# First expert's products in halves, a reordered tail and earlier records in a retention and mixture-of-experts kernel

## Chip, cores and metric

One core of a Trainium2 chip runs the whole program. The metric is the device time of one execution in microseconds; lower is better. Before the change it is 412.31 us (median of 3 runs, 411.94 to 412.67).

## What is computed

The reference first runs a retention (decayed linear attention) over 4 batches, 8 heads, 768 positions and 64 features, and then a mixture of experts in which each of the 3072 rows of 512 features goes to the one expert with the largest logit:

```python
intra = (qb @ kb^T * Dmask) @ vb ; inter = (qb * lam_pow) @ kv_state
kv_state = lam_block * kv_state + kb_dec^T @ vb
x = out.transpose(0, 2, 1, 3).reshape(3072, 512)
logits = x @ w_gate ; e_idx = argmax(logits)
for e in range(8):
    h = relu(x[e_idx == e] @ w1[e])          # 512 -> 1024
    out[e_idx == e] = gate_w * eom[:, e] * (h @ w2[e])   # 1024 -> 512
```

`gate_w` is the softmax weight of the chosen expert and `eom` a sigmoid of a second gate.

## The kernel before

The rows are cut into 24 tiles of 128 (six chunks of positions by four batches, `NTILE = 24`, `B = 4`, `RES = 16`, `LAST = 20`). A loop over steps `s` runs the retention of one tile a step, software-pipelined: `stage_a` turns keys and queries on TensorE, `stage_b` and `stage_b2` make the decayed scores, `stage_c1` and `stage_c` make the output x (`xT`, features on partitions) and the state, and `stage_d2` turns x back with VectorE and stores it to `x_d` in device memory. The order of instructions is the order of the Python calls (`tc.manual_schedule`), on each engine's queue.

Routing runs beside it by groups of tiles: `logits` (TensorE), `logit_rows` (a transpose and, for the last two groups, a sum `lg`), `route_choose` (VectorE: `mx`, `pl`, `cm`, `oh`; then two exponentials on ScalarE and the *record* of each row on GpSimd, an `IOTA` and a `TENSOR_SCALAR` that write the row's number and its place in `x_d` into `rec`), and `route_place` (rank products `pr` on TensorE, then about eleven small VectorE steps that end in the slot `sl`, the index `idx` and the weight in `rec`). `place_scatter` writes each tile's records to a table in device memory, `tab_d`, with one indirect DMA of GpSimd per tile. The groups are four tiles each up to tile 19, then tiles 20 and 21 (`LAST`), then 22 and 23 (`LAST + 2`).

The expert with the most rows so far is found before the last tiles are done (`pick_first`, from the counts of the first 16 tiles), so its weights load early: `load_piece(i)` loads the i-th piece of 1 MB, pieces 0 and 1 being the halves of its first matrix, 2 and 3 those of the second (`raw`). Rows of that expert come in two ways. Those of the first 16 tiles come from `tab_d` and a search (`mark`, `found`, `row_turn`, `row_index`, `row_join`) and are gathered in steps 18 to 21 by eight indirect DMAs of GpSimd, 32 rows each (`gather(0, ...)`, line 894; tiles `xg_0`, `xg_1`, four gathers each). Ahead of every second gather stands a hold, `pace`, a copy of one element of `xT` to `beat` on GpSimd (line 841). The remaining rows of the expert come in six gathers at the end (`xg_2`, `xg_3`), behind the late search `pfound_late`. `x_turn(0, i)` turns a tile `xg_i` on VectorE into `y` (line 911).

The first expert's products are a list of 48 `units`: 32 products of `up_mm` (8 column blocks `fc` by 4 feature blocks `kc`, line 945, 128x128 weights from `raw` against the 256 columns of `y_0`, in plain float32, two matmul records each) and 16 of the second matrix. `fill(n)` takes the next n units and `settle(n)` runs the relu steps (`up_act`) of completed blocks. The tail after the loop, from line 1302, interleaves both with the last routing by hand; its lines before the first expert's own loop are:

```python
x_turn(0, 0); logits(LAST + 2, 2); x_turn(0, 1); stage_d2(n - 3, 2)
load_piece(2); fill(3)
for f in place[1:]: f()
place_scatter(len(pending)); logit_rows(LAST + 2); fill(6)
```

Behind the six late gathers the second piece of the first expert's rows (`ys[(0, 1)]`, 192 columns) is multiplied, again at line 945, and from there on TensorE runs one expert after the other. PSUM has eight banks, taken in turn (`bank`).

Of the kernel before, what the change touches and what calls it, by code (L numbers as in the profile page):

```python
# [9 lines left out]
F32 = mybir.dt.float32  # L10
# [13 lines left out]
def kernel(  # L24
# [446 lines left out]
    def logits(n0, nb):  # L471
        parts = P // EG // nb
        pl = bank(f"pl_{n0}")
        for i in range(NPAIR // parts):
            for b in range(nb):
                xTv = xTs.pop((n0 + b)) if i == NPAIR // parts - 1 else xTs[n0 + b]
                xTv = xTv.rearrange("p (g t) -> p g t", g=NPAIR)
                for k in range(parts):
                    g = k * (NPAIR // parts) + i
                    r = (b * parts + k) * EG  # L480
                    nc.tensor.matmul(
                        pl[r : r + EG, 0:P], wgs[:, g, :], xTv[:, g], start=(i == 0), stop=(i == NPAIR // parts - 1)
                    )
        lT = small.tile([P, P], F32, tag="lT", name=f"lT_{n0}")
        nc.scalar.copy(out=lT, in_=pl[:, 0:P])
        lgs[n0] = (pl, lT, nb, parts)
# [41 lines left out]
    routed = {}  # L528

# [9 lines left out]
    def route_choose(n0, n1):  # L539
# [21 lines left out]
        rec = sm("rec", [P, nb, 3], I32)  # L561
# [6 lines left out]

        def record():
            nc.gpsimd.iota(rec[:, :, 0], pattern=[[S, nb]], base=b0 * S + c * P, channel_multiplier=1)  # L570
            nc.gpsimd.tensor_scalar(
                out=rec[:, :, 2], in0=row0[:, b0 : b0 + nb], scalar1=float(c * B * P * 4), scalar2=None,
                op0=ALU.add,
            )
# [9 lines left out]
            lambda: (exps(), record()),  # L584
# [353 lines left out]
    def up_mm(p, fc, h, kc):  # L938
        sl = slice((fc % 4) * P, (fc % 4 + 1) * P)
        r = cols(p, h)  # L940
        if kc == 0:
            phs[(p, fc)] = bank(f"ph_{p}_{fc}_{h}")
        if p == 0:
            nb = min(8, NB[p] - 8 * h)
            nc.tensor.matmul(  # L945
                phs[(p, fc)][:, r].rearrange("p (b r) -> p b r", b=nb),
                raws[fc // 4][:, kc, sl],
                ys[(p, h)][:, 0 : nb * P].rearrange("p (b g r) -> p g b r", b=nb, g=NPAIR)[:, kc],
                start=(kc == 0),
                stop=(kc == NKC - 1),  # L950
            )
            return
# [223 lines left out]
    for fc in range(NFC):  # L1176
        for kc in range(NKC):
            act = (lambda fc=fc: up_act(0, fc, 0)) if kc == NKC - 1 else None
            units.append((lambda fc=fc, kc=kc: up_mm(0, fc, 0, kc), act))
# [16 lines left out]
    with tc.manual_schedule():  # L1196
        ranking = []
        late = []
        STORES = {4: 0, 6: 2, 8: 4, 9: 6, 11: 8, 13: 10, 14: 12, 16: 14, 20: 16, 21: 18}
# [9 lines left out]
        for s in range(-2, NTILE - 2):  # L1209
# [64 lines left out]
            if s == 5:  # L1274
                number_tables()
            if s >= 0:
# [14 lines left out]
            if s >= RES + 2:  # L1291
                pace(xTs[s][0:1, 0:1])
# [3 lines left out]
                if s == RES + 5:  # L1296
                    load_rows(0, 2, None, nc.gpsimd)
                    load_piece(1, nc.gpsimd)
            if s < RES:
# [24 lines left out]
        x_turn(0, 1)  # L1324
        stage_d2(n - 3, 2)
        load_piece(2)
        fill(3)
        for f in place[1:]:
            f()
        place_scatter(len(pending))  # L1330
        logit_rows(LAST + 2)
        fill(6)
        at_once(route_choose(LAST + 2, NTILE))
        for b in range(2):
            mark(LAST, b, 1, late_width)
        last = route_place(LAST + 2, NTILE)
        counts = rank_counts("pcount")
        last[0]()
        fill(6)
# [4 lines left out]
        for b in range(2):  # L1344
            mark(LAST + 2, b, 1, late_width)
        pfound = bank("pfound_late")
        for n in range(RES, NTILE):
            found(pfound, n, (n - RES) // B + 1, late_width, n == RES, n == NTILE - 1)
        settle(2)
# [3 lines left out]
        fill(5)  # L1353
        row_turn(2, pfound, late_width)
        row_index(0, 2)
# [41 lines left out]
        for p in range(E):  # L1397
# [5 lines left out]
            for fc in range(NFC):  # L1403
# [21 lines left out]
                if p == 0 and fc < 2:  # L1425
                    next_rows(1, 10 + 2 * fc, 12 + 2 * fc, hts[(p, fc)][0][0:1, 256:257].bitcast(F32))
# [196 lines left out]
```

## Time and profile before

| | before |
|---|---|
| median of 3 runs | 412.31 us (411.94 to 412.67) |
| the profiled execution | 413.83 us |
| its span, first to last instruction | 412.2 us |
| TensorE (PE) busy | 397.1 us, 96% |
| VectorE (DVE) busy | 280.3 us, 68% |
| ScalarE (ACT) busy | 184.0 us, 45% |
| GpSimd (POOL) busy | 233.0 us, 57% |
| mean granted clock of TensorE | 0.993 |

The profile is of one execution. Times in its rows are microseconds from the start of the span unless marked ns; a row of the timeline has the start, the length, the engine, the line of the kernel, the operation, the output and inputs, how many instructions are merged (x), and in brackets the idle time before it and what ended that. A busy TensorE also counts time in which a product runs at a lower clock, so the clock is read apart, in the views by stretch.

### The profile page before, as it was taken

To read this page: it belongs to the slowest core of one execution; us is meant where nothing else is said; L and a number is where in the kernel's file an instruction comes from. 1 tells how busy PE (TensorE), PEld (TensorE's weight loads), DVE (VectorE), ACT (ScalarE), POOL (GpSimd) and SP (SyncE) were. 2 spreads that over 40 slices of the span, in tenths; PEclk is the share of its full clock that TensorE was granted. 3 is DMA by queue.
4 is the path that set the end of the run, shared out by engine and by line. 5 is a ranking of instruction groups with operands and counts; after the bars stand their busy time and mean duration, and the time that the engine had idled before them with its cause. 6 is when DMAs were issued, how large, how long until landed. Compare 5 with 4: busy or idle time off the path is not lost.

```text
span 412.2 us, 10314 instructions
## 1 busy us (share of the span) xinstructions
PE 397.1 (96%) x3767; PEld 364.2 (88%) x3767; DVE 280.3 (68%) x798; ACT 184.0 (45%) x450; POOL 233.0 (57%) x305
## 2 busy tenths in 40 slices
PE   8999989799969999999999999999999999999995
PEld 5879978688858898999999999999999989989985
DVE  3858786678867639778669757957965874863611
ACT  3757656578413325446045325604713542542500
POOL 2567877755876777874583666376386266211002
PEclk9999999999989999999999999999999999999998
DMA  9999999998968844744369648757946985461001
GB/s 179 225 206 254 230 220 233 254 224 198 286 196 249 242 164 105 241 147 139 127 185 308 220 130 237 242 183 188 320 151 172 300 258 167 129 214 64 0 26 48
DMA packets 102116, 78.96 MB, mean 192 GB/s; under 512 B 66348, under 2 KB 78128, under 8 KB 102064
## 3 DMA queue, kind: packets, MB, share of 16 engines
q1 hardware_dynamic: 93264, 63.85, 55.5%
q0 software_dynamic: 6544, 14.15, 11.1%
q10 hardware_dynamic: 2256, 0.30, 0.5%
q8 instruction: 30, 0.49, 0.5%
q14 instruction: 22, 0.18, 0.2%
HBM read 62.45 MB, written 16.21 MB: 191 GB/s over the span
## 4 chain that ended last, share of the span: by engine, by line
PE 75%; DMA 12%; SPq 6%; DVE 3%; issue 1%; POOL 1%; ACTq 0%; POOLq 0%; DVEq 0%
PE ph_None L83 10%; PE ph_None L82 10%; PE ph_None L81 10%; PE py L82 6%; PE py L83 6%; PE py L81 6%; PE pyr L82 4%; PE pyr L81 4%; PE pyr L83 4%; SPq L175 3%; PE ps L389 3%; PE ph L945 3%; SPq L168 3%; DMA tab_d<-rec,idx 3%; PE po L433 2%; DMA xg<-x_d,rows 2%
## 5 line engine op out<-in xcount | busy, mean ns | idle before, releaser
L894 POOL DMA_INDIRECT xg<-x_d,rows x103 | 114.5, 1112 | 63.7 <-issue 34.7
L971 ACT ACTIVATE hhi<-ph_None 128x400 fp32r<-128x400 f32 (+4 forms) x56 | 28.1, 501 | 120.5 <-PE ph_None L83 115.6
L136 DVE TENSOR_TENSOR wlo<-raw,whi 128x512 fp32r<-128x512 f32 x120 | 79.6, 684 | 0.7 <-ACT whi L127 0.5
L83 PE MATMUL ph_None<-xhi,wlo 128*128 128x400 f32 (+4 forms) x224 | 76.3, 341 | 0.0
L81 PE MATMUL ph_None<-xhi,whi 128*128 128x400 f32 (+4 forms) x224 | 76.3, 341 | 0.0
L82 PE MATMUL ph_None<-xlo,whi 128*128 128x400 f32 (+4 forms) x224 | 76.3, 341 | 0.0
L127 ACT CAST whi<-raw 128x512 fp32r<-128x512 f32 x120 | 70.0, 614 | 0.0
L977 DVE SCALAR_TENSOR_TENSOR hlo<-ph_None,hhi 128x400 fp32r<-128x400 f32 (+4 forms) x56 | 31.8, 568 | 37.2 <-ACT hhi L971 37.0
L398 DVE TENSOR_TENSOR at<-ps,decay 128x512 f32<-128x512 f32 x48 | 31.2, 683 | 22.5 <-PE ps L389 22.2
L83 PE MATMUL py<-hhi,wlo 128*128 128x400 f32 (+2 forms) x128 | 44.6, 348 | 0.0
L82 PE MATMUL py<-hlo,whi 128*128 128x400 f32 (+2 forms) x128 | 44.6, 348 | 0.0
L81 PE MATMUL py<-hhi,whi 128*128 128x400 f32 (+2 forms) x128 | 44.6, 348 | 0.0
L81 PEld LDWEIGHTS ph_None<-xhi,whi 128*128 128x128 f32 x224 | 42.1, 188 | 0.4
L82 PEld LDWEIGHTS ph_None<-xlo,whi 128*128 128x128 f32 x224 | 42.1, 188 | 0.4
L83 PEld LDWEIGHTS ph_None<-xhi,wlo 128*128 128x128 f32 x224 | 42.1, 188 | 0.3
L1092 POOL DMA_INDIRECT out_dram<-yn,table x12 | 13.3, 1112 | 49.5 <-DVE yn L1165 31.9
L349 ACT COPY qT<-pq 64x256 f32<-64x256 f32 x88 | 34.7, 394 | 2.5 <-PE pq L341 1.7
L81 PE MATMUL pyr<-whi,hhi 128*128 128x512 f32 (+1 forms) x88 | 34.6, 393 | 0.0
L82 PE MATMUL pyr<-wlo,hhi 128*128 128x512 f32 (+1 forms) x88 | 34.3, 390 | 0.0
L83 PE MATMUL pyr<-whi,hlo 128*128 128x512 f32 (+1 forms) x88 | 34.3, 390 | 0.0
L699 POOL DMA_INDIRECT tab_d<-rec,idx x24 | 24.6, 1024 | 14.9 <-DVE rows L853 4.5
L945 PE MATMUL ph<-y,raw 128*128 128x256 f32 (+1 forms) x128 | 26.9, 369 | 3.4 <-issue 3.2
(211 smaller groups left out, 717.2 us busy)
## 6 DMA issues: line engine op xcount, KB each, us to landing
raw<-in_moe_w_dram SPq DMA_DIRECT2D x31, 1024.0 KB
x_d<-xn SPq DMA_DIRECT2D x12, 512.0 KB
qkv<-in_k_dram SPq DMA_DIRECT2D x38, 128.0 KB
qkv<-in_v_dram SPq DMA_DIRECT2D x19, 256.0 KB
qkv<-in_q_dram SPq DMA_DIRECT2D x36, 128.0 KB
yd<-yo SPq DMA_DIRECT2D x12, 256.0 KB
yr<-yd SPq DMA_DIRECT2D x48, 64.0 KB
xg<-x_d,rows POOLq DMA_INDIRECT x103, 3.4
```

The costliest lines, as they stand in the source:

```text
L81: nc.tensor.matmul(ps, a[0], b[0], start=first, stop=False)
L82: nc.tensor.matmul(ps, a[0], b[1], start=False, stop=False)
L83: nc.tensor.matmul(ps, a[1], b[0], start=False, stop=last)
L127: nc.scalar.copy(out=hi, in_=src)
L136: eng.tensor_tensor(out=lo, in0=src, in1=hi.bitcast(F32), op=ALU.subtract)
L349: copies = [lambda r=r, view=view, src=src: nc.scalar.copy(out=view(qT[r]), in_=src) for r, view, src in query_parts(pq)]
L398: nc.vector.tensor_tensor(out=at, in0=ps.rearrange("p (g t) -> p g t", g=NPAIR), in1=dec[:, j], op=ALU.mult)
L699: nc.gpsimd.indirect_dma_start(out=tab_d, out_offset=bass.IndirectOffsetOnAxis(ap=idx, axis=0), in_=rec, in_offset=None, bounds_check=P * ...
L894: nc.gpsimd.indirect_dma_start(out=xg[(p, b // 4)][:, (b % 4) * P : (b % 4 + 1) * P], out_offset=None, in_=x_q[0 : 4 * rows], in_offset=ba ...
L945: nc.tensor.matmul(phs[(p, fc)][:, r].rearrange("p (b r) -> p b r", b=nb), raws[fc // 4][:, kc, sl], ys[(p, h)][:, 0 : nb * P].rearrange(" ...
L971: nc.scalar.activation(out=hi[:, r], in_=ph[:, r], func=AF.Relu)
L977: nc.vector.scalar_tensor_tensor(out=to, in0=ph[:, r], scalar=0.0, in1=hi[:, r].bitcast(F32), op0=ALU.max, op1=ALU.subtract,)
```

## The change

Five things are changed. The first 16 of the first expert's products are issued as 32 products of 128 columns: the halves that need `xg_0` alone first, then those of `xg_1`. The tail is put in another order. The records of the groups of tiles 12, 16, 20 and 22 are made in steps 6, 7, 9 and 10, in tiles of their own (`rec_...` in `const`). Piece 2 of the weights, which Sync loaded in the tail, is loaded by GpSimd directly behind piece 1. The holds at the early gathers and at the last four gathers of the second expert are removed. `lT` also gets one buffer in place of two.

```diff
-        lT = small.tile([P, P], F32, tag="lT", name=f"lT_{n0}")
+        lT = small.tile([P, P], F32, tag="lT", bufs=1, name=f"lT_{n0}")
...
+    recs = {}
+    def record(rec, n0, nb):
+        c, b0 = divmod(n0, B)
+        nc.gpsimd.iota(rec[:, :, 0], pattern=[[S, nb]], base=b0 * S + c * P, channel_multiplier=1)
+        nc.gpsimd.tensor_scalar(
+            out=rec[:, :, 2], in0=row0[:, b0 : b0 + nb], scalar1=float(c * B * P * 4), scalar2=None, op0=ALU.add
+        )
+    def early_record(n0, nb):
+        recs[n0] = const.tile([P, nb, 3], I32, name=f"rec_{n0}")
+        record(recs[n0], n0, nb)
...
-            lambda: (exps(), record()),
+            lambda: (exps(), None if known else record(rec, n0, nb)),
...
-    def up_mm(p, fc, h, kc):
+    def up_mm(p, fc, h, kc, part=None):
...
+            if part is not None:
+                nb, y0, r = 4, 4 * P * part, slice(P * part, P * part + P)
...
-    for fc in range(NFC):
-        for kc in range(NKC):
-            act = (lambda fc=fc: up_act(0, fc, 0)) if kc == NKC - 1 else None
+    for part, fcs in ((0, range(4)), (1, range(4)), (None, range(4, NFC))):
+        for fc in fcs:
+            for kc in range(NKC):
+                act = (lambda fc=fc: up_act(0, fc, 0)) if kc == NKC - 1 and part != 0 else None
...
+        EARLY_RECORDS = {6: (RES - B, B), 7: (RES, B), 9: (LAST, 2), 10: (LAST + 2, 2)}
...
+            if s in EARLY_RECORDS:
+                early_record(*EARLY_RECORDS[s])
...
             if s >= RES + 2:
-                pace(xTs[s][0:1, 0:1])
                 gather(0, 2 * (s - RES - 2) + 1, 2 * (s - RES - 2) + 2, RES * P)
...
                     load_piece(1, nc.gpsimd)
+                    load_piece(2, nc.gpsimd)
...
         logits(LAST + 2, 2)
-        x_turn(0, 1)
-        stage_d2(n - 3, 2)
-        load_piece(2)
-        fill(3)
+        fill(8)
         for f in place[1:]:
             f()
-        place_scatter(len(pending))
-        logit_rows(LAST + 2)
-        fill(6)
-        at_once(route_choose(LAST + 2, NTILE))
         for b in range(2):
             mark(LAST, b, 1, late_width)
+        place_scatter(len(pending))
+        x_turn(0, 1)
+        logit_rows(LAST + 2)
+        fill(8)
+        at_once(route_choose(LAST + 2, NTILE))
+        stage_d2(n - 3, 2)
         last = route_place(LAST + 2, NTILE)
+        fill(4)
         counts = rank_counts("pcount")
         last[0]()
-        fill(6)
+        fill(4)
         stage_d2(n - 1, 2)
         load_piece(3)
...
             mark(LAST + 2, b, 1, late_width)
+        fill(10)
         pfound = bank("pfound_late")
...
-        settle(2)
...
         place_scatter(len(pending))
-        fill(5)
+        settle(1)
+        row_index(0, 2)
+        fill(2)
         row_turn(2, pfound, late_width)
-        row_index(0, 2)
         row_join(2, late_width)
...
-                    next_rows(1, 10 + 2 * fc, 12 + 2 * fc, hts[(p, fc)][0][0:1, 256:257].bitcast(F32))
+                    next_rows(1, 10 + 2 * fc, 12 + 2 * fc)
```

On TensorE, at the end of the last logits (`pl`) and the start of the first expert's products (`ph_0` is block 0, `y_0` holds eight gathered pieces), before:

```order
L481 MATMUL pl_2607<-xT_2565,wgs 32x128 x2
L945 MATMUL ph_0_0_2625<-y_0_2605,raw_2390 128x256 x3
L492 MATMUL pl_2607<-ident,lT_2616 128x128
L945 MATMUL ph_0_0_2625<-y_0_2605,raw_2390 128x256
L945 MATMUL ph_1_0_2651<-y_0_2605,raw_2390 128x256 x4
L945 MATMUL ph_2_0_2656<-y_0_2605,raw_2390 128x256
```

and with the change:

```order
L481 MATMUL pl_2608<-xT_2569,wgs 32x128 x2
L953 MATMUL ph_0_0_2619<-y_0_2606,raw_2394 128x128 x4
L953 MATMUL ph_1_0_2624<-y_0_2606,raw_2394 128x128 x4
L492 MATMUL pl_2608<-ident,lT_2617 128x128
L953 MATMUL ph_2_0_2654<-y_0_2606,raw_2394 128x128 x4
L953 MATMUL ph_3_0_2659<-y_0_2606,raw_2394 128x128 x4
L953 MATMUL ph_0_0_2619<-y_0_2606,raw_2394 128x128 x4
```

Sixteen half products of blocks 0 to 3 now stand ahead of the first that needs the second four pieces, and eight instead of three products stand ahead of the transpose of the last logits.

On VectorE, at the turns of `xg_0` and `xg_1` into `y_0`, before:

```order
L583 TENSOR_TENSOR oh_2461<-pl_2530,cm_2584 128x16
L911 STREAM_TRANSPOSE y_0_2605<-xg_0_2153 128x512
L911 STREAM_TRANSPOSE y_0_2605<-xg_1_2373 128x512
L516 STREAM_TRANSPOSE xn_2619<-xT_2379 128x512
L516 STREAM_TRANSPOSE xn_2619<-xT_2468 128x512
L672 TENSOR_REDUCE pr_2601<-ex_2585 128x2
```

and with the change, from the end of the placing of tiles 20 and 21 (which now follows the turn of `xg_0` at once):

```order
L672 RECIPROCAL rec_1191<-den_2598 128x2
L651 TENSOR_REDUCE oh_2639<-oh_2464 128x8
L601 TENSOR_SCALAR marks_2641<-slot_no,lead_142,sl_2599 128x192 x2
L917 STREAM_TRANSPOSE y_0_2606<-xg_1_2377 128x512
L496 TENSOR_REDUCE lg_2652<-pl_2608 128x32
L583 TENSOR_REDUCE mx_2664<-lg_2652 128x2
L584 TENSOR_TENSOR pl_2608<-lg_2652,mx_2664 128x16
L585 SCALAR_TENSOR_TENSOR pl_2608<-pl_2608,erev 128x16
L588 TENSOR_REDUCE cm_2665<-pl_2608 128x2
L589 TENSOR_TENSOR oh_2639<-pl_2608,cm_2665 128x16
L516 STREAM_TRANSPOSE xn_2675<-xT_2383 128x512
```

The turn of `xg_1` moved behind the placing and the marks of tiles 20 and 21, and the x transposes moved behind the choosing for tiles 22 and 23.

On GpSimd, from the load of piece 1 on (`DMASW0` to `DMASW7` are the semaphores of its DMAs, each used by every eighth one in turn, so that a DMA waits for the landing of the one eight places ahead; `tab_d<-rec,idx` is a scatter), before:

```order
L114 DMA raw_2485<-in_moe_w_dram 128x4x512 [waits DMASW2_49]
L699 DMA tab_d<-rec_2358,idx_2372 24576x3 [waits DMASW3_49,DMASW1_49,DVE_49]
L699 DMA tab_d<-rec_2358,idx_2372 24576x3
L841 COPY beat<-xT_2565 1x1 [waits Activation_49,Pool_49]
L699 DMA tab_d<-rec_2358,idx_2372 24576x3 [waits DMASW5_49]
L699 DMA tab_d<-rec_2358,idx_2372 24576x3 [waits DMASW6_49]
L570 IOTA rec_2587 128x2
L571 TENSOR_SCALAR rec_2587<-row_136 128x2
L699 DMA tab_d<-rec_2587,idx_2600 24576x3 [waits DMASW7_49,DVE_49,Pool_49]
L699 DMA tab_d<-rec_2587,idx_2600 24576x3 [waits DMASW0_49]
L570 IOTA rec_2662 128x2
L571 TENSOR_SCALAR rec_2662<-row_136 128x2
```

and with the change, to the last scatter:

```order
L114 DMA raw_2487<-in_moe_w_dram 128x4x512 [waits DMASW2_49]
L114 ISA
L114 DMA raw_2489<-in_moe_w_dram 128x4x512 [waits DMASW3_49]
L705 DMA tab_d<-rec_955,idx_2376 24576x3 [waits DMASW1_49,DVE_49]
L705 DMA tab_d<-rec_955,idx_2376 24576x3 [waits DMASW5_49]
L847 COPY beat<-xT_2569 1x1 [waits Activation_49,Pool_49]
L705 DMA tab_d<-rec_955,idx_2376 24576x3 [waits DMASW6_49]
L705 DMA tab_d<-rec_955,idx_2376 24576x3 [waits DMASW7_49]
L705 DMA tab_d<-rec_1191,idx_2601 24576x3 [waits DMASW0_49,DVE_49]
L705 DMA tab_d<-rec_1191,idx_2601 24576x3
L705 DMA tab_d<-rec_1282,idx_2682 24576x3 [waits DMASW2_49,DVE_49]
L705 DMA tab_d<-rec_1282,idx_2682 24576x3 [waits DMASW3_49]
```

Both records left the row of scatters, a second weight piece stands ahead of it, and the first scatter waits in both for the semaphore DMASW1, that of the small read of `index_2` from `tab_d` just ahead of the weights; the last scatter now has the semaphore DMASW3, used last by piece 2.

## Rows read from the trace of the kernel before

**Rows 1.** The page: its first line.

```profile
span 412.2 us, 10314 instructions
```

**Rows 2.** The waits of TensorE from 100 us on: in total, times, longest.

```profile
PE ph L945 <- issue: 3.2, 1, 3.2
```

**Rows 3.** Timeline of TensorE, 100 to 160 us.

```profile
114.30 0.65 PE L481 MATMUL pl<-xT,wgs 128*32 128x128 f32 x16
118.17 1.57 PE L945 MATMUL ph<-y,raw 128*128 128x256 f32 x6 [3.23 <-issue]
...
126.76 0.25 PE L602 MATMUL pfound_late<-marks,row_lo 128*128 128x192 bf16 x1
...
128.08 7.53 PE L945 MATMUL ph<-y,raw 128*128 128x256 f32 x34
...
146.69 10.64 PE L945 MATMUL ph<-y,raw 128*128 128x192 f32 x64 [0.15 <-DVE y L911]
```

**Rows 4.** The chain that ended last, 100 to 160 us: start, length, what.

```profile
114.76 2.58 DMA xg<-x_d,rows
...
138.44 7.63 DMA xg<-x_d,rows
```

**Rows 5.** Timeline of VectorE, 100 to 160 us.

```profile
114.10 0.71 DVE L911 STREAM_TRANSPOSE y<-xg 128x512 f32<-128x512 f32 x1
...
118.00 1.26 DVE L516 STREAM_TRANSPOSE xn<-xT 128x512 f32<-128x512 f32 x2
...
120.47 0.21 DVE L496 TENSOR_REDUCE lg<-pl 128x32 f32<-128x64 f32 x1
...
121.56 0.17 DVE L583 TENSOR_TENSOR oh<-pl,cm 128x16 bf16<-128x16 f32 x1
...
124.27 0.18 DVE L663 TENSOR_TENSOR pr<-pr,ebase 128x16 f32<-128x16 f32 x1 [0.85 <-PE pr L633]
...
125.40 0.74 DVE L977 SCALAR_TENSOR_TENSOR hlo<-ph,hhi 128x256 fp32r<-128x256 f32 x2
...
129.50 0.23 DVE L876 TENSOR_TENSOR rows<-found,rows 128x4 int32<-128x4 f32 x2
...
146.10 0.45 DVE L911 STREAM_TRANSPOSE y<-xg 128x256 f32<-128x256 f32 x1 [3.60 <-DMA xg<-x_d,rows]
```

**Rows 6.** Busy time by stretch: length, PE, PEld, DVE, ACT, POOL, granted clock, DMA share, GB/s.

```profile
119.00:123.00 4.00, 4.00 (x13) 3.22 (x12) 3.76 (x22) 0.69 (x3) 3.23 (x5) 0.57 1.12 378
...
118.00:132.00 14.00, 13.83 (x72) 11.91 (x73) 10.79 (x54) 3.24 (x9) 9.60 (x14) 0.88 0.99 297
20.00:60.00 40.00, 38.60 (x854) 34.00 (x851) 28.34 (x90) 25.20 (x69) 30.45 (x48) 1.00 0.96 231
```

**Rows 7.** The same chain as rows 4, transposes of queries.

```profile
100.68 0.44 PE pq L341 x4
```

**Rows 8.** Timeline of GpSimd, 96 to 172 us.

```profile
109.64 0.74 POOL L571 TENSOR_SCALAR rec<-row 128x4 int32<-128x4 f32 x1
...
114.42 0.18 POOL L841 COPY beat<-xT 1x1 f32<-1x1 f32 x1
114.76 1.02 POOL L894 DMA_INDIRECT xg<-x_d,rows  x1 [0.16 <-DMA tab_d<-rec,idx]
...
116.44 0.84 POOL L114 DMA_DIRECT2D raw<-in_moe_w_dram  x1
118.65 1.07 POOL L699 DMA_INDIRECT tab_d<-rec,idx  x1 [1.37 <-DVE y L911]
...
129.09 0.99 POOL L699 DMA_INDIRECT tab_d<-rec,idx  x1 [0.30 <-issue]
131.37 1.07 POOL L894 DMA_INDIRECT xg<-x_d,rows  x1 [1.29 <-DVE keys L745]
```

**Rows 9.** Timeline of Sync's queue, 96 to 172 us.

```profile
134.54 4.22 SPq L114 DMA_DIRECT2D raw<-in_moe_w_dram  x2
```

**Rows 10.** DMA issues from 124 to 127 us: count, median us to landing.

```profile
tab_d<-rec,idx POOLq DMA_INDIRECT x2, 8.0
```

More of the change, by code (lines that the diff above doesn't have):

```diff
@@ L560, in route_choose @@
         ex, ez = sm("ex", [P, nb, E]), sm("ez", [P, nb, E])
-        rec = sm("rec", [P, nb, 3], I32)
+        rec = recs.pop(n0) if n0 in recs else sm("rec", [P, nb, 3], I32)
+        known = n0 >= RES - B
         routed[n0] = (oh, ex, ez, rec)
@@ L567, in exps @@
             nc.scalar.activation(out=ex, in_=d, func=AF.Exp)
[L569 to L574, printed above, removed]
         return [
@@ L936 @@
     hts = {}
-    def up_mm(p, fc, h, kc):
+    def up_mm(p, fc, h, kc, part=None):
         sl = slice((fc % 4) * P, (fc % 4 + 1) * P)
         r = cols(p, h)
-        if kc == 0:
+        if kc == 0 and not part:
             phs[(p, fc)] = bank(f"ph_{p}_{fc}_{h}")
         if p == 0:
-            nb = min(8, NB[p] - 8 * h)
+            nb, y0 = min(8, NB[p] - 8 * h), 0
+            if part is not None:
+                nb, y0, r = 4, 4 * P * part, slice(P * part, P * part + P)
             nc.tensor.matmul(
@@ L947, in up_mm @@
                 raws[fc // 4][:, kc, sl],
-                ys[(p, h)][:, 0 : nb * P].rearrange("p (b g r) -> p g b r", b=nb, g=NPAIR)[:, kc],
+                ys[(p, h)][:, y0 : y0 + nb * P].rearrange("p (b g r) -> p g b r", b=nb, g=NPAIR)[:, kc],
                 start=(kc == 0),
@@ L1175 @@
     acts = []
-    for fc in range(NFC):
-        for kc in range(NKC):
-            act = (lambda fc=fc: up_act(0, fc, 0)) if kc == NKC - 1 else None
-            units.append((lambda fc=fc, kc=kc: up_mm(0, fc, 0, kc), act))
+    for part, fcs in ((0, range(4)), (1, range(4)), (None, range(4, NFC))):
+        for fc in fcs:
+            for kc in range(NKC):
+                act = (lambda fc=fc: up_act(0, fc, 0)) if kc == NKC - 1 and part != 0 else None
+                units.append((lambda fc=fc, kc=kc, part=part: up_mm(0, fc, 0, kc, part), act))
     for j in range(2):
```

## The prediction

> **What bounds the kernel now.** I start with the page: the span is 412.2 us [rows 1]; the profiled execution took 413.83 us, so 1.6 us lie outside the span. The list of TensorE's waits comes next. From 100 us to the end it names one idle time worth a step, 3.2 us before the first expert's products (line 945) [rows 2]; the only other at that line is 0.15 us before their second piece, at 146.69 [rows 3]. Behind that the list has nothing: one unbroken stream of products, so whatever moves the start of the second piece moves the end by as much, as long as nothing later runs dry.
>
> The timeline of TensorE shows the hole: the last logits start at 114.30 us and end near 114.9, and the first product starts at 118.17 [rows 3]. It waited for the *second* half of its 256 rows: a product takes 8 gathered pieces at once, pieces 4 to 7 landed at 117.34 [rows 4], and VectorE turned them then, while the first four had been turned from 114.10 to 114.81 [rows 5]. Then the clock: from 119 to 123 us the granted clock is 0.57 on average, that is 1.2 of 2.4 GHz for most of it [rows 6]. Before it fell, the engine had stood idle for those 3.2 us and had been busy again for about one. So 4 x 0.43 = 1.7 us more are lost there.
>
> But TensorE is one of two chains that meet at 146.69. The other is the second piece of rows: its last gather is issued at 138.44 and lands 7.63 us later [rows 4], VectorE turns it at 146.10 [rows 5], and TensorE goes on 0.15 us after it had run out of other work. Both chains must become shorter, or the gain of the first is lost at the second.
>
> **The change part by part.** *Halves.* The first 16 products become 32 of 128 columns, and the first 16 of those need only the turn that ends at 114.81. TensorE starts at 114.9 instead of 118.17: **-3.3 us**. Without that idle time I expect the clock to stay up: **-1.7 us**. Each half loads its weights again. Rows on both sides: the four 128-column products of a transpose take 0.44 us, 0.11 each [rows 7], and the 34 records of 256 columns 7.53 us, 0.22 each [rows 3] (a product is two records). By these two halves cost what one whole does, and I take 0. The dear end is that a half record is no cheaper than one of 192 columns, 10.64 / 64 = 0.166 us [rows 3]: 64 x 0.166 - 32 x 0.22 = +3.6 us. I stay at the cheap end because the 0.11 is measured on the same 128 columns with a new 128x128 load for each. The Trainium skill (TensorE: Matmul & The Clock Gate, Back-to-back issue gap) speaks against the halves: in a stream of load and product it gives about 81 ns for 128 columns where the product alone would take 56. By that factor of 1.45 the halves would cost about 3 us more, an estimate from that page; rows 7 do not show it. TensorE would now run out of other work at 146.54 - 3.3 - 1.7 = **141.6 us**.
>
> *Reordered tail, VectorE.* The turn of pieces 4 to 7 goes behind the placing of the last-but-one pair of tiles and its marks. Laid out by durations: the placing takes 1.2 us (119.26 to 120.47 [rows 5]) and ends at 116.0, the marks at 116.6, the turn at 117.3, the choosing (120.47 to 121.73 [rows 5]) at 118.6, four x transposes at 0.63 each [rows 5] at 121.1, three placing steps and marks (124.27 to 125.40 [rows 5]) at 122.3. TensorE needs the turn at 114.9 + 16 x 0.22 = 118.4 and the marks at about 123.2: a margin near 1 us in both places. The 16 "found" products take 1.3 us (126.76 to 128.08 [rows 3]) and end at 124.5; the row numbers, ready at 129.73 before [rows 5], come at about 125.4, over 4 us earlier. The first x store moves 0.7 us back, to 120, the second 2.2 us forward, to 121.2; both are before the gathers by far more than they need.
>
> *Holds and records, GpSimd.* The removed one-element copies hold nothing back: the one at 114.42 starts as its gather ends and the next gather follows 0.34 us behind that, where two DMAs in a row stand 0.30 apart [rows 8]. I cost them at nothing. The record of tile group 16 took 0.74 us of arithmetic plus its index fill between two gathers [rows 8]; without it the last of the early gathers moves from 114.76 [rows 8] to about 113.7. The eight late scatters start from 118.65 to 129.09 [rows 8], 10.4 us for seven steps, where a scatter of 0.99 and a gap of 0.30 [rows 8] would make 9.1: the two records between them cost 1.3 us. Their new place is in steps 6 to 10, where GpSimd has 30.5 busy us in 40 and TensorE waits for others [rows 6]; I cost them at nothing, and at most 4 x 0.9 us if TensorE had to wait for each.
>
> *Weight piece 2 on GpSimd's queue.* It adds a 0.84 us issue there [rows 8]. In its favour, the next scatter waits anyway, as the order shows, for the small index read; the raw issue ended at 117.28 and the scatter started at 118.65 [rows 8]. The index read moves forward with the gathers, so the first scatter comes at about 117.5 and the last at 129.09 - 1.15 - 1.3 = 126.6. SP loses one issue and its next piece is no longer behind piece 2. That is later than the row numbers (125.4): GpSimd's queue is **late next**. From the last scatter to the first gather went 2.28 us, 129.09 to 131.37 [rows 8], of which 1.0 has no releaser that I can name. With it the gather chain moves by 2.45 us, without it by 3.4. Its landing is the unknown: 2.58 us when nothing else is in flight, 7.63 when a weight piece issued at 134.54 and the next one 4 us later run beside it [rows 4, 9]. SP's pieces move forward too, since they wait for the scatters and for buffers that TensorE's pace frees, so the race stays about as it was. At 7.63 the second piece starts at 143.3 to 144.2; at 2.58 it starts when TensorE is ready, at 141.6. I take 143.2, near the middle: 146.69 - 143.2 = **3.5 us gained**. The single buffer for lT costs nothing; its two uses are 3 us apart.
>
> The sum against the profiled execution: 413.83 - 3.5 = 410.3. The median of the runs is 412.31, 1.5 lower, so **408.8 us**.
>
> **The rivals.** (A) *The halves are dear.* At the 192-column price, +3.6 us, TensorE arrives at 145.2, behind the gathers: 412.3 - 1.5 = 410.8. For it: each half loads its weights anew; against it: the 0.11 us of rows 7. Chance 0.08.
> (B) *The clock falls all the same*, at the wait of up to 2 us that is left before the second piece, or in the tail: 1.7 us come back, 410.5. For it: it fell once after an idle time [rows 6]; against: that one was longer. Chance 0.10.
> (C) *The change does not do what it says*, because the weight piece is dear on GpSimd: from 116.44 to 118.65 went 2.21 us [rows 8], and if that was the issue itself and not the index read, piece 2 adds 2.2 us. Then the last scatter is at 128.8, close to before, the gathers hardly move, TensorE waits for them, and the time is about 412. Chance 0.12.
> (D) *Slower.* The scatters share a queue with 2 MB of weights, and the last one waits, as the order shows, for the landing of piece 2 (DMASW3). From 118 to 132 us 297 GB/s were moved [rows 6], 4.2 MB: about three weight pieces and two x stores. If piece 2 is served last, it lands at 117.3 + 14 = 131.3. Then the last scatter is at 131.6, the first gather 2.28 later, the last 7.07 behind that at 141.0, and it lands at 148.6: TensorE starts at 149.2, 2.5 us later than now, 414.8, and 1.7 more if the clock falls. It decides from the point at which the last gather lands behind 146.1 us. For it: scatters took 8.0 us to land beside such traffic [rows 10]. Against: pieces 1 and 2 are issued before the x stores and have a head start of 3 us. Chance 0.07. The Trainium skill (DMA: Bandwidth & Descriptors, Issuing engine by pattern and Arbitration) also speaks against this edit: plain loads belong on Sync, and an engine takes turns between queues but serves one queue in order. By that rule the scatters land behind both pieces; this trace, with only piece 1 on that queue, cannot show the second.
>
> **How the numbers follow.** My forecast has 0.63, with a range of its own from 407.3 (TensorE ready at 141.6, everything landed) to 409.9 (2.45 us gained). With A and B the range is **407.3 to 411.0**; C and D, 0.19, lie outside. A measurement here tells apart about 0.2%, 0.8 us. Faster by more: 0.63 + 0.08 + 0.10 and a part of C, 0.84. Within it: most of C, 0.09. Slower: D, 0.07.
>
> **What would show it.** Right: the first product of line 945's kind starts within 0.3 us of 114.9, no stretch of 119 to 123 below a clock of 1, half records 0.11 us apart, the last scatter near 127, the first late gather near 128 to 129, and the second piece at 142 to 144. Wrong: half records of 0.16; a gap of 2 us behind each weight issue on GpSimd; the last gather landing behind 146; a TensorE wait of over 2 us ahead of the second piece; or a new wait of TensorE on GpSimd between 35 and 60 us, where the records now stand.

## The result and the profile after

| | before | after |
|---|---|---|
| median, same chip | 414.4 us (411.94 to 416.38, 20 runs) | 412.99 us (407.26 to 418.42, 20 runs) |
| ratio | | 0.9916 (0.9888 to 0.9943) |
| the profiled execution | 413.83 us | 414.16 us |
| its span | 412.2 us | 412.6 us |

The ratio leaves out executions more than 1.5% above their kernel's fastest: here 9 of the 20 of the changed kernel and none of the kernel before, in the third group below 16 of 24 of the kernel before. On the 412.31 us that the prediction started from it makes 408.85 us (407.7 to 410.0). With all 20 executions the quotient of the two medians is 0.9966, which makes 410.9 us. The profiled execution is one of the longer ones of the changed kernel, and that is useful here: it shows what the gain is lost to when it is lost.

The list of TensorE's waits of the changed kernel (us in total, times, longest):

```profile
PE ph L953 <- DVE y L917: 3.5, 1, 3.5
```

The 3.2 us ahead of the first product [rows 2] are gone, and a wait of 3.5 us stands ahead of the second piece instead. The timeline of TensorE has both places:

```profile
113.12 1.12 PE L481 MATMUL pl<-xT,wgs 128*32 128x128 f32 x16
114.36 2.02 PE L953 MATMUL ph<-y,raw 128*128 128x128 f32 x16
...
116.32 2.84 PE L953 MATMUL ph<-y,raw 128*128 128x128 f32 x24
...
119.16 3.79 PE L953 MATMUL ph<-y,raw 128*128 128x128 f32 x28
...
145.44 6.79 PE L953 MATMUL ph<-y,raw 128*128 128x192 f32 x30 [3.54 <-DVE y L917]
```

The first half product starts right behind the last logits; 24 half records go by in the 2.68 us from 116.32 to 119.00, 0.11 us each. TensorE had run out of other work at 145.44 - 3.54 = 141.9 and stood until VectorE had turned the last rows:

```profile
113.54 0.71 DVE L917 STREAM_TRANSPOSE y<-xg 128x512 f32<-128x512 f32 x1 [0.63 <-DMA xg<-x_d,rows]
116.05 0.69 DVE L917 STREAM_TRANSPOSE y<-xg 128x512 f32<-128x512 f32 x1
124.72 0.23 DVE L882 TENSOR_TENSOR rows<-found,rows 128x4 int32<-128x4 f32 x2
139.45 0.71 DVE L917 STREAM_TRANSPOSE y<-xg 128x512 f32<-128x512 f32 x1 [2.21 <-DMA xg<-x_d,rows]
144.85 0.45 DVE L917 STREAM_TRANSPOSE y<-xg 128x256 f32<-128x256 f32 x1 [4.68 <-DMA xg<-x_d,rows]
```

The row numbers are there at 124.95, 4.8 us earlier than before [rows 5], but the last turn comes only 1.25 us earlier (144.85 against 146.10). The timeline of GpSimd says where the rest went (the first row is the last early gather, then the small index read, the two weight pieces, the first and last late scatter, the first and last late gather), and Sync's two rows give the issues of weight pieces 4 and 5 together, and that of piece 5 alone:

```profile
112.06 1.00 POOL L900 DMA_INDIRECT xg<-x_d,rows  x1 [0.30 <-issue]
114.58 0.65 POOL L830 DMA_DIRECT2D index<-tab_d  x1 [1.52 <-DMA tab_d<-rec,idx]
115.22 1.57 POOL L114 DMA_DIRECT2D raw<-in_moe_w_dram  x2
118.49 1.07 POOL L705 DMA_INDIRECT tab_d<-rec,idx  x1 [1.70 <-DVE oh L589]
...
127.58 1.10 POOL L705 DMA_INDIRECT tab_d<-rec,idx  x1 [0.30 <-issue]
130.30 1.05 POOL L900 DMA_INDIRECT xg<-x_d,rows  x1 [1.61 <-DVE wlo L136]
...
137.86 1.00 POOL L900 DMA_INDIRECT xg<-x_d,rows  x1 [0.30 <-issue]
...
133.72 4.22 SPq L114 DMA_DIRECT2D raw<-in_moe_w_dram  x2
...
137.55 0.38 SPq L114 DMA_DIRECT2D raw<-in_moe_w_dram  x1
```

The last late gather goes out at 137.86 (138.44 before) and its rows are turned 7.0 us later, as before with its 7.6 [rows 4]. The view by stretches (busy time of each engine, then the granted clock, the DMA share and GB/s) shows what fills those 7 us and what follows:

```profile
119.00:123.00 4.00, 4.00 (x39) 3.80 (x37) 3.77 (x19) 1.54 (x4) 3.23 (x5) 1.00 0.89 284
142.00:146.00 4.00, 0.56 (x3) 0.59 (x4) 1.08 (x2) 0.00 (x0) 3.09 (x4) 1.00 0.96 238
146.00:148.00 2.00, 2.00 (x9) 2.00 (x8) 0.00 (x0) 0.18 (x1) 1.66 (x2) 0.50 0.85 312
148.00:150.00 2.00, 2.00 (x10) 2.00 (x9) 0.42 (x2) 0.16 (x2) 1.42 (x2) 0.64 0.17 57
```

The clock is 1.00 from 119 to 123 (0.57 before [rows 6]). It falls to 0.50, 1.2 of 2.4 GHz, behind the new wait: 2 x 0.50 + 2 x 0.36 = 1.7 us. So in this execution what was won in front, some 5 us, is paid again 30 us later: 3.5 us in the wait and 1.7 by the clock.

### The profile page after: what moved, and what is told of

Same layout as the page of the kernel before. It is cut to its first block, busy times and chain, and to the rows that moved or that the text cites. A ratio compares the mean times of both kernels' runs of the same rounds, so it can differ in the third digit from the quotient of the medians.

```text
span 412.6 us, 10361 instructions
## 1 busy us (share of the span) xinstructions
PE 397.3 (96%) x3799; PEld 365.4 (89%) x3799; DVE 280.1 (68%) x798; ACT 184.9 (45%) x450; POOL 231.1 (56%) x300
## 4 chain that ended last, share of the span: by engine, by line
PE 74%; DMA 12%; DVE 4%; SPq 3%; POOL 3%; issue 2%; ACT 0%; ACTq 0%; POOLq 0%; DVEq 0%
PE ph_None L82 10%; PE ph_None L83 10%; PE ph_None L81 10%; PE py L82 6%; PE py L83 6%; PE py L81 6%; PE pyr L82 4%; PE pyr L83 4%; PE pyr L81 4%; DMA qkv<-in_q_dram 4%; PE ph L953 3%; DMA raw<-in_moe_w_dram 3%; PE ps L389 2%; DMA xg<-x_d,rows 2%; PE po L433 2%
## 5 line engine op out<-in xcount | busy, mean ns | idle before, releaser
L900 POOL DMA_INDIRECT xg<-x_d,rows x103 | 112.7, 1094 | 66.4 <-issue 33.2
L953 PE MATMUL ph<-y,raw 128*128 128x128 f32 (+2 forms) x160 | 27.1, 331 | 3.7 <-DVE y L917 3.5
```

The source lines that it names most:

```text
L900: nc.gpsimd.indirect_dma_start(out=xg[(p, b // 4)][:, (b % 4) * P : (b % 4 + 1) * P], out_offset=None, in_=x_q[0 : 4 * rows], in_offset=ba ...
L953: nc.tensor.matmul(phs[(p, fc)][:, r].rearrange("p (b r) -> p b r", b=nb), raws[fc // 4][:, kc, sl], ys[(p, h)][:, y0 : y0 + nb * P].rearr ...
```

## The experiments

Two theories beside the prediction's own. **R**: the last late gather races with the weight pieces 4 and 5, and where it lands behind them TensorE waits and then loses the clock. **S**: the first late gather waits for the landing of the last x store, which stands behind weight pieces 1 and 2; by the prediction's theory, **Q**, GpSimd's queue alone sets it. Twelve runs were made, in three groups of four; each group shares a chip, and each ratio is to the kernel before on that chip.

### First group

**The changed kernel again**, no edit.

> The changed kernel once more, unaltered, as the measure for the other runs of this chip. Theory R (a race: the last of the late gathers of the first expert lands before or behind the two weight pieces that Sync loads at 133.7 and 137.9 us, and TensorE waits for it): the single times spread over 5 us or more, from about 407 to 418, and in the profile the wait of TensorE ahead of its second piece of rows lies between 0 and 4 us, with a fall of the granted clock behind it when it is over 3. Theory N (the spread is the chip's and not the kernel's): the kernel before spreads as much on the same chip.

Measured: 414.78 us (412.33 to 418.47, 12 runs), ratio 0.9972 (0.9936 to 1.0008). The kernel before took 415.7 us here, with as wide a spread (413.32 to 419.53): here the spread does not belong to the change, while on the first chip the changed kernel spread over 11.2 us and the kernel before over 4.4. The gain on this chip is 0.3%, and the interval takes in none at all. The wait that R expects is there, 3.57 us (its row stands further down), and so is the fall of the clock behind it:

```profile
148.00:150.00 2.00, 2.00 (x8) 2.00 (x8) 0.33 (x1) 0.00 (x0) 1.39 (x3) 0.59 0.55 200
```

**Pieces 4 and 5 held back.**

```diff
+        if held_back:
+            nc.vector.memset(raws[i][0:1, 0, 0:1], 0.0)
...
-        load_piece(4)
         expert_regs(2, order_i[:, 2:E], E - 2)
-        load_piece(5)
...
         for i in range(2, 4):
             x_turn(0, i)
+        for i in (4, 5):
+            load_piece(i, held_back=True)
```

The write of one element makes each load wait until VectorE, in its order, has turned the last rows.

> The fourth and fifth weight pieces (raw 4 and raw 5) are issued only when VectorE has turned the last gathered rows, so that nothing large is in flight beside the late gathers. Theory R (race): the last late gather lands within about 3 us of its issue at 137.9, TensorE goes on at about 142 with a wait under 0.5 us and no fall of the clock; the times gather near 407 (406.5 to 408.5) and their spread falls to 2 us or less. Theory S (the landing is set by pieces 1 to 3 and the x stores, not by pieces 4 and 5): the last landing stays near 144.8, the wait stays over 2 us, the time stays near 411 to 413. A third outcome: the weights come too late for the second expert and a wait of TensorE of 1 us or more appears between 150 and 170 us; then about 409 to 411.

Measured: 410.61 us (410.12 to 415.56, 6 runs, four of them below 410.9), ratio 0.9863 (0.9821 to 0.9905), which on 412.31 is 406.7. The views of its profile, first GpSimd's last late gather and VectorE's two turns (line numbers are two higher here), then the stretches:

```profile
139.69 1.20 POOL L902 DMA_INDIRECT xg<-x_d,rows  x1 [0.31 <-issue]
...
143.96 1.03 DVE L919 STREAM_TRANSPOSE y<-xg 128x512 f32<-128x512 f32 x2
...
118.91 3.75 PE L955 MATMUL ph<-y,raw 128*128 128x128 f32 x16 [1.60 <-DMA raw<-in_moe_w_dram]
...
148.53 3.74 PE L955 MATMUL ph<-y,raw 128*128 128x192 f32 x22
```

```profile
119.00:123.00 4.00, 4.00 (x19) 4.00 (x20) 0.80 (x2) 0.00 (x0) 1.60 (x3) 0.50 0.95 312
...
142.00:146.00 4.00, 4.00 (x19) 3.34 (x18) 1.74 (x6) 0.00 (x0) 2.61 (x3) 1.00 0.19 41
146.00:148.00 2.00, 2.00 (x10) 1.65 (x10) 0.00 (x0) 0.00 (x0) 1.38 (x3) 1.00 0.75 209
148.00:150.00 2.00, 2.00 (x14) 1.88 (x13) 0.75 (x1) 0.00 (x0) 1.70 (x2) 1.00 1.04 400
```

With 41 GB/s in flight in place of 238, the last turn follows the first at once and waits for no landing, 4.9 us behind the issue of the gather; the second piece starts with no idle time and at a clock of 1.00. This profiled execution is the longest of the six for another reason: its first product waited 1.60 us for weight piece 0, and the clock was 0.50 from 119 to 123. That makes it a poor witness for the missing wait: TensorE came to the second piece at 148.53, 8.8 us behind the issue of the gather, and would not have waited for one that was turned after 6.7 to 7.9 us either. What speaks for R is the median, 4.2 us below the changed kernel's with intervals of the ratios that do not meet, and the landing of the gather: the traces hold the time at which each DMA has landed, though the views here do not print it, and the last late gather landed at 143.23, 3.5 us after its issue. The profile shows no later wait for the held pieces. The time is not as low as R expected on the first chip's scale (406.5 to 408.5), and the six spread over 5.4 us and not 2.

**Piece 2 back on Sync**, behind both x stores.

```diff
                     load_piece(1, nc.gpsimd)
-                    load_piece(2, nc.gpsimd)
...
         stage_d2(n - 1, 2)
+        load_piece(2)
         load_piece(3)
```

> Weight piece 2 goes back from GpSimd's queue to Sync's, behind both x stores instead of between them. Theory S (the first late gather waits for the landing of the last x store, which stands behind the weight pieces 1 and 2 on their way): the last x store lands earlier, the first late gather starts at 127 to 128.5 instead of 130.3, although the row numbers and the last scatter hardly move; TensorE's wait shrinks by up to 2 us and the median falls by 1 to 3 us. Theory Q (GpSimd's queue sets the first late gather, as the prediction had it): GpSimd saves one issue of about 0.8 us, and the first late gather moves by that at most, to about 129.5; the median falls by less than 1 us.

Measured: 411.46 us (410.13 to 412.59, 6 runs), ratio 0.987 (0.9832 to 0.9907). Rows of its timelines (the last late scatter, the first and last late gather, the last turn, Sync's pieces 4 and 5 together and piece 5 alone, the second piece):

```profile
130.53 0.97 POOL L705 DMA_INDIRECT tab_d<-rec,idx  x1 [0.30 <-issue]
131.81 1.06 POOL L900 DMA_INDIRECT xg<-x_d,rows  x1 [0.31 <-issue]
...
139.21 0.99 POOL L900 DMA_INDIRECT xg<-x_d,rows  x1 [0.30 <-issue]
...
143.20 0.45 DVE L917 STREAM_TRANSPOSE y<-xg 128x256 f32<-128x256 f32 x1 [1.53 <-DMA xg<-x_d,rows]
...
137.39 4.20 SPq L114 DMA_DIRECT2D raw<-in_moe_w_dram  x2
141.21 0.38 SPq L114 DMA_DIRECT2D raw<-in_moe_w_dram  x1
...
145.55 4.71 PE L953 MATMUL ph<-y,raw 128*128 128x192 f32 x28
```

The first late gather came at 131.81, where S had 127 to 128.5 and Q at most 129.5, because everything in front came later; it follows the last scatter by 0.31 us, and nothing but the queue holds it. But the gain comes from the other end: Sync issues pieces 4 and 5 later by 2.5 us than in the changed kernel beside it, piece 5 at 141.21, 2.0 us behind the last gather; in the first profile piece 5 went out at 137.55, 0.3 us ahead of the gather. So only piece 4 is ahead of it, the gather is turned 4.0 us after its issue, and TensorE does not wait, although it comes to the second piece 6.3 us behind that issue. So the median falls by 3.3 us, more than either theory on the first gather would give. The start of that gather does not settle S here: the changed kernel run beside it,

```profile
130.24 0.97 POOL L705 DMA_INDIRECT tab_d<-rec,idx  x1 [0.30 <-DVE ranked L791]
131.51 1.33 POOL L900 DMA_INDIRECT xg<-x_d,rows  x1 [0.30 <-issue]
...
139.38 0.99 POOL L900 DMA_INDIRECT xg<-x_d,rows  x1 [0.30 <-issue]
...
147.25 0.45 DVE L917 STREAM_TRANSPOSE y<-xg 128x256 f32<-128x256 f32 x1 [5.51 <-DMA xg<-x_d,rows]
...
147.84 4.36 PE L953 MATMUL ph<-y,raw 128*128 128x192 f32 x15 [3.57 <-DVE y L917]
```

has the 0.30 us too, because its scatters started 2.6 us later than in the first profile (121.10).

The landings in the traces settle it. In the first profile the last x store was issued at 120.32 and landed at 129.35; GpSimd's queue stood in its wait for that landing until 129.38, and the gather started 0.9 us later, at 130.30. Before the change the store landed at 130.43 and the gather started at 131.37, again 0.9 us later; with pieces 4 and 5 held back and with the halves undone it is the same 0.9. In the other two profiles (129.33 and 131.51, 128.42 and 131.81) the store had landed 2.2 and 3.4 us before the gather, and the queue came last. So S and Q are both right, each in a part of the executions: the later of the store's landing and the queue sets the gather.

**The halves undone**, the rest of the change kept.

```diff
-    for part, fcs in ((0, range(4)), (1, range(4)), (None, range(4, NFC))):
+    for part, fcs in ((None, range(NFC)),):
...
-        fill(8)
```

(and the later counts from 4, 4 and 10 to 2, 2 and 6.)

> The halves alone are undone: the first 16 products take all 256 columns again and stand behind the turn of pieces 4 to 7; the rest of the change stays. If the gathers set the second piece (R or S): TensorE waits about 2.5 to 3.3 us near 115 us, the clock may fall there, but the second piece still starts within 0.5 us of where it does in the changed kernel on this chip, and the median moves by less than 1 us. If TensorE's own work sets it: the second piece and the end come 3 to 5 us later, near 412 to 414 in all runs.

Measured: 414.91 us (411.06 to 417.51, 12 runs), ratio 0.9953 (0.9917 to 0.999), against 414.78 and 0.9972 with halves. In its timelines:

```profile
119.69 4.55 PE L953 MATMUL ph<-y,raw 128*128 128x256 f32 x20 [1.82 <-issue]
...
146.63 0.45 DVE L917 STREAM_TRANSPOSE y<-xg 128x256 f32<-128x256 f32 x1 [4.45 <-DMA xg<-x_d,rows]
147.22 4.95 PE L953 MATMUL ph<-y,raw 128*128 128x192 f32 x29 [1.01 <-DVE y L917]
```

The second piece starts no later than with halves (147.22 against 147.84), behind the gathers, and no gain of the halves shows in the time. The first product starts 3.1 us later (119.69 against 116.63), but this is not the price of undoing them: the last logits and the first product with halves beside it,

```profile
114.36 0.64 PE L481 MATMUL pl<-xT,wgs 128*32 128x128 f32 x16
116.63 2.02 PE L953 MATMUL ph<-y,raw 128*128 128x128 f32 x16 [1.63 <-DVE marks L601]
```

and the last logits with the halves undone,

```profile
116.43 0.65 PE L481 MATMUL pl<-xT,wgs 128*32 128x128 f32 x16
```

are 2.1 us apart already. The first half product had waited too: the profile names VectorE's marks, but it starts 0.1 us behind the landing of weight piece 0 at 116.50. From the last logits to the end of its other work TensorE took 29.9 us with halves and 29.8 without. So this pair says that the halves saved nothing on TensorE in these executions; what they save where piece 0 is there in time was not measured alone.

The six profiles in one table, from the rows above, those of before [rows 3 to 5], their neighbours in the same views and, for the landing of the last gather, the traces. Whatever lies in front, the end follows the start of the second piece by 265.4 to 265.6 us, plus 1.7 to 1.9 where the clock fell (behind the wait of 1.01 us, with the halves undone, it stayed at 1.00):

| | first product | other work done | piece 5 issued | last gather issued | landed | turned | second piece | from there to the end |
|---|---|---|---|---|---|---|---|---|
| before | 118.17 | 146.54 | 138.37 | 138.44 | 146.08 | 146.10 | 146.69 | 265.5 |
| after | 114.36 | 141.90 | 137.55 | 137.86 | 144.75 | 144.85 | 145.44 | 267.2 |
| after, second chip | 116.63 | 144.27 | 138.71 | 139.38 | 147.16 | 147.25 | 147.84 | 267.3 |
| pieces 4, 5 held | 118.91 | 148.53 | 146.01 | 139.69 | 143.23 | 144.6 | 148.53 | 265.4 |
| piece 2 on Sync | 118.23 | 145.55 | 141.21 | 139.21 | 143.18 | 143.20 | 145.55 | 265.5 |
| halves undone | 119.69 | 146.21 | 138.55 | 139.96 | 146.54 | 146.63 | 147.22 | 265.6 |

Where piece 5 is issued ahead of the gather, by 0.07 to 1.41 us, the gather lands 6.6 to 7.8 us after its issue; where it is issued behind it, 3.5 and 4.0. The eight profiles of the later groups agree: with a piece issued 0.41 us ahead (late records) the gather took at least 7.3 us, in the other seven, with none in the 2 us ahead, 3.2 to 5.0. So the race is decided by which of the two is issued first. Why a piece ahead costs the gather that much is not shown.

### Second group

These fell on a chip where everything, the kernel before included (433.56 us, 427.8 to 439.01, 11 runs), takes some 5% longer. **Both edits together** (pieces 4 and 5 held, piece 2 on Sync), and **both with the halves undone**, the diffs as above:

> Both edits that helped alone: weight piece 2 behind the x stores on Sync, and pieces 4 and 5 issued only behind the turn of the last gathered rows. If each removes its own wait (the landing of the last x store ahead of the first late gather; the weights ahead of the last gather's landing), no wait of TensorE is left before its second piece, no clock falls, and the times lie at or below those of either edit alone: a ratio to the kernel before of 0.98 to 0.987. If the two edits act on the same wait (the queueing of the last gather), the ratio is that of one alone, 0.986 to 0.988.

> The same, with the halves undone as well, so that TensorE stands idle for some 2 to 3 us until the turn of pieces 4 to 7. If TensorE's own work now sets the second piece, as the prediction had it at best (3.3 us for the start and 1.7 for the clock), the time is 3 to 5 us above the version with halves: a ratio of 0.99 to 0.998. If the gathers still set it, the two agree within 1 us.

Measured: 436.97 us, ratio 1.0123 (1.0054 to 1.0193), and 438.75 us, ratio 1.0205 (1.0144 to 1.0266). **The late records** (the table of early records emptied) and **the holds put back**:

```diff
-        EARLY_RECORDS = {6: (RES - B, B), 7: (RES, B), 9: (LAST, 2), 10: (LAST + 2, 2)}
+        EARLY_RECORDS = {}
```

```diff
             if s >= RES + 2:
+                pace(xTs[s][0:1, 0:1])
                 gather(0, 2 * (s - RES - 2) + 1, 2 * (s - RES - 2) + 2, RES * P)
...
-                    next_rows(1, 10 + 2 * fc, 12 + 2 * fc)
+                    next_rows(1, 10 + 2 * fc, 12 + 2 * fc, hts[(p, fc)][0][0:1, 256:257].bitcast(F32))
```

> The changed kernel with the records of the last four tile groups made late again, two of them between the late scatters on GpSimd. By the prediction's theory (GpSimd's queue is what the late gathers wait for) the last late scatter moves back by 1.3 us against the first of them, 10.4 us for the seven steps instead of 9.1, and the last of the early gathers by about 1; the median rises by 1 to 2 us. By theory S (the x store's landing sets the first late gather) the gather follows the last scatter by 0.3 to 1 us instead of 2.7, starts where it did, and the median moves by less than 0.7 us.

> The changed kernel with the one-element holds ahead of the gathers put back. The prediction cost them at nothing: early gathers 0.34 us behind the one before instead of 0.30, and the time within 0.5 us of the changed kernel's. A rival: the holds set when the early gathers of the first expert start beside the loads of q, k and v, and without them the loads that TensorE waits for come later or earlier; then the time moves by over 1 us and the waits of TensorE for q, k and v between 95 and 115 us differ by as much.

Measured: 436.43 us, ratio 1.0126 (1.004 to 1.0211), and 438.99 us, ratio 1.0169 (1.0097 to 1.024). The changed kernel itself was not in this group, the four intervals overlap, and the times expected of the edits are not to be read from them: inconclusive. One thing can be read inside a profile. With late records, between two late scatters:

```profile
133.08 0.97 POOL L706 DMA_INDIRECT tab_d<-rec,idx  x1 [0.31 <-issue]
134.06 0.16 POOL L534 IOTA rec<- 128x2 int32 x1
134.29 0.22 POOL L535 TENSOR_SCALAR rec<-row 128x2 int32<-128x2 f32 x1
134.80 1.03 POOL L706 DMA_INDIRECT tab_d<-rec,idx  x1 [0.29 <-issue]
```

A record makes 0.75 us of the usual 0.30 between two scatters, 0.45 us for each of the two.

### Third group

The same again beside the changed kernel; it fell on another chip that is as long (before 437.26 us, 429.64 to 441.29, 24 runs).

> The changed kernel, unaltered, on whatever chip this call gets, as the measure for the three runs beside it. Theory R (race of the last gather with weight pieces 4 and 5): a spread of 5 us or more, and a wait of TensorE of 2 to 4 us ahead of its second piece in the profile. The ratio to the kernel before lies between 0.990 and 1.000 on a chip like the first two.

> Weight piece 2 back on Sync behind both x stores, once more. If the second chip told truly, this is 0.7 to 1.0% below the changed kernel on the same chip, with half its spread, and TensorE has no wait over 1 us ahead of its second piece.

> Piece 2 on Sync behind the x stores, and pieces 4 and 5 held until the last gathered rows are turned; its first runs fell on a chip where every engine stood without instructions for some 10 us, so that nothing could be read from the time. If each edit removes its own wait: at or below either alone, a ratio to the kernel before of 0.98 to 0.987. If they act on the same wait: 0.986 to 0.988, like one alone.

> The same with the halves undone. If TensorE's own work sets the second piece once the gathers are early, the time is 3 to 5 us above the version with halves; if the gathers still set it, the two agree within 1 us.

| | median | ratio |
|---|---|---|
| changed kernel | 441.03 us | 1.0243 (1.0186 to 1.0301) |
| piece 2 on Sync | 443.0 us | 1.0154 (1.0066 to 1.0243) |
| both edits | 444.05 us | 1.0154 (1.0071 to 1.0237) |
| both, halves undone | 440.26 us | 1.0108 (1.0026 to 1.019) |

No time came as expected: here the change is slower than the kernel before, by 0.9% by the medians, and the orders of medians and of ratios contradict each other among the variants. The race does not show here: in all four profiles the last gather lands 3.3 to 5.0 us after its issue and TensorE has no wait before its second piece, the changed kernel's own included, so the two edits had nothing to remove. In the profile of the changed kernel, TensorE's waits from 95 to 130 us, and a few rows of its timeline there:

```profile
PE pl L481 <- issue: 6.5, 14, 0.8
```

```profile
109.05 0.29 PE L481 MATMUL pl<-xT,wgs 128*32 128x128 f32 x1 [0.45 <-issue]
...
110.51 0.64 PE L481 MATMUL pl<-xT,wgs 128*32 128x128 f32 x4 [0.45 <-issue]
111.92 0.65 PE L481 MATMUL pl<-xT,wgs 128*32 128x128 f32 x4 [0.78 <-issue]
```

One set of 32 logits products, 1.08 us in the first profile, goes from 104.67 to 116.86, 12.2 us; it has 14 stalls, 6.5 us with the 0.3 of the one just ahead of it, that wait for nothing the profile shows; the first half product starts at 131.94, 17.6 us later than in the first profile. Undoing the halves there moved the median by +1.8 us in the second group and by -3.8 in the third, so the halves are not shown to be the cause. Two more waits stand behind the logits that the first profile does not have, 3.0 us for ScalarE's `whi` and 2.1 us at `pcount`. Why the change loses on these chips stays open: no profile of the kernel before was taken there. The words "every engine stood without instructions for some 10 us" (`best_b`) say more than the profile that they speak of: there TensorE's idle times without a releaser add up to 11 us over the whole run, and GpSimd was busy for 12.9 of the 20 us from 100 to 120.

## Why the prediction came out right, and where it was wrong

**The time.** 408.8 was forecast, with 407.3 to 411.0; the ratio gives 408.85 (407.7 to 410.0). That it meets the centre is in part luck: with all executions it is 410.9, and on the second chip 0.9972 gives 411.2 (409.7 to 412.6), both at the range's upper end. The forecast stands between two outcomes, a gather that lands early and one that lands late, and the profiles show the one or the other. It holds for chips like these two; on that of the third group the sign is the other one, and no rival had a cause for that.

**Halves and start: right in this execution.** The first product starts at 114.36, 0.5 us ahead of the 114.9 forecast, right behind logits that began 1.2 us earlier than before (113.12 against 114.30 [rows 3]); on the second chip weight piece 0 held it up by 1.6 us, a wait that the prediction did not have. Half records of 0.11 us were forecast and measured, so rival A falls. By an estimate from the figures of the Trainium skill (TensorE: Matmul & The Clock Gate, Back-to-back issue gap) the halves would have been about 3 us dearer; the trace does not agree: at 0.11 us each, two half records take what one whole one did [rows 3].

**The clock in front: right**, 1.00 from 119 to 123. **Rival B was right too, in the profiled execution**: the clock fell at the wait before the second piece and 1.7 us came back. The wait was 3.5 us and not the up to 2 that B had.

**TensorE out of other work at 141.6, row numbers at 125.4: right in number**, 141.9 and 124.95, with the help of logits that began 1.2 us earlier than before. Counted from the logits, TensorE's chain gained 3.5 us of the 5.0 forecast. **Scatters: right** for the records (seven steps in 127.58 - 118.49 = 9.09 us, 9.1 forecast); the last one came at 127.6 instead of 126.6, since the first began 1 us later than forecast.

**Piece 2 on GpSimd**: the two issues take 1.57 us together, 0.8 each as forecast, so rival C falls. Rival D falls as well: the first late scatter follows the index read, at 118.49, and the last is not held to 131: piece 2 landed at 124.56 in place of D's 131.3. The first scatter did land behind it, at 126.37. **Records and holds at nothing:** TensorE has no wait on GpSimd between 20 and 100 us, where the records now stand, and was busy for 39.98 us of the 40 from 20 to 60; the holds were put back on a chip where nothing can be read, so their term is not shown.

**The step that failed** is the gather chain, "With it the gather chain moves by 2.45 us, without it by 3.4", and with it "x stores ... before the gathers by far more than they need". The wait that had no name is the landing of the last x store: the store was issued 3.1 us earlier (120.32 against 123.45) but took 9.0 us to land in place of 7.0, so it landed 1.08 earlier, and the first late gather moved by 1.07, to 130.30 in place of the forecast 128 to 129. By GpSimd's queue alone, with the usual 0.30 behind the last scatter, it would have come at 128.98. The last late scatter moved by 1.51 us; the gathers themselves took 7.56 us to the last in place of 7.07, so that moved by 0.58; and the last turn by 1.25. TensorE's chain gained 4.6 us, 1.2 of them in front of the logits, this one a quarter of that. By the prediction's own signs the second piece (145.44, 142 to 144 forecast) and TensorE's wait of 3.5 us (over 2 was to be a sign of being wrong) speak against it.

**The unknown that was named decides the size.** The landing of the last gather was given 2.58 to 7.63 us and set near the middle. It is not a middle but a race: 6.6 to 7.8 us to the landing where piece 5 was issued up to 1.4 us ahead of it, 4.0 where it was issued 2.0 us behind it, and 3.5 where both pieces were held. "The race stays about as it was" was right, and it was the sentence with the most money in it: the gain in front can only be kept where the gather wins. Removing the race was worth 1.1% on the second chip (0.9863 against 0.9972), several times what the change alone was worth there; the edit was not run alone on another chip.

## What to carry to other kernels

Where two chains meet, shortening one is worth at most the slack of the other: look at what the other waits for at its very end, here a gather of 64 KB (32 rows of 512 numbers) behind weights that nobody needed yet. Before work is brought forward, hold back the large transfers that are not due, by a tie to the work that they would disturb; that one edit gave more on the chip where both were measured than halves, reordering and early records together. A gain of 1% that rests on who wins a race has to be measured on more than one chip.

## What the runs showed that was not expected

- A gather of 64 KB landed 6.6 to 7.8 us after its issue where a 1 MB piece of Sync was issued up to 1.4 us ahead of it, and after 3.2 to 5.0 us in the nine profiles without one; the bytes moved do not tell it alone: with piece 4 ahead and piece 5 behind it, at 286 GB/s from 142 to 146, it took 4.0.
- An x store issued 3.1 us earlier landed only 1.1 us earlier (9.0 us behind its issue in place of 7.0): moving an issue forward did not move the landing by as much. Why it took longer is not shown.
- The first product of the changed kernel's family starts anywhere from 114.36 to 118.91 us with nearly the same instructions in front: TensorE's waits for q, k, v, weight piece 0 and without a releaser vary by that much from one execution to the next, more than the whole effect of the change.
- Two of the four chips run all kernels, the one before too, some 5% longer. In the changed kernel's profile there TensorE stands still 14 times within 12 us in the middle of the logits, for nothing that the profile shows; on the second chip the same line shows one such stall of 1.0 to 1.4 us in two of four profiles.
